# Two attention branches on one core: scaling phi(Q) on GpSimd in place of dividing numerators on VectorE

## The chip, the cores and the metric

The kernel runs on one core of a Trainium2 chip. The metric is the device time of one execution in microseconds (us). A core has five engines that each run their own stream of instructions in order: TensorE (PE, with the loading of weights as PEld), VectorE (DVE), ScalarE (ACT), GpSimd (POOL) and SyncE (SP), which here issues DMAs. They wait for each other through semaphores: `s_pe`, `s_dve`, `s_act` and `s_pool` count an engine's finished work, and `s_n5`, `s_n6`, `s_q0` and their like count landed DMAs.

## The reference, cut to what matters

Input x is 2048 x 512 with 32 heads of 16. Branch A is softmax attention. Branch B is linear attention with phi. A gate per token mixes them.

```python
g = sigmoid((x * gate_w).sum(-1, keepdims=True))
# A
scores = einsum("bhqd,bhkd->bhqk", q, k) * Dh ** -0.5
a = (softmax(scores) @ v) @ A_wo
# B: phi(t) = where(t > 0, t + 1, exp(t)) + 1e-6
kv = einsum("bhsd,bhse->bhde", phi(k), v)
z = einsum("bhsd->bhd", phi(k))
num = einsum("bhqd,bhde->bhqe", phi(q), kv)
den = einsum("bhqd,bhd->bhq", phi(q), z)[..., None] + 1e-6
b = (num / den) @ B_wo
return g * a + (1 - g) * b
```

## The kernel before, in words

**Branch A** is 32 rounds (a group of 8 heads, a quarter of 512 queries, and one of two halves of the heads) of 64 units each. A unit is the scores of 128 keys by 512 queries for one head. TensorE makes the scores in PSUM (`ps<-Qpad,KT`), and there are two ways on. ScalarE exponentiates two or three units with one instruction (`PT<-ps`, 128x1024 or 128x1536), and each result goes into one product with V (`ps<-PT,Vaug`). Or VectorE converts one unit to a 16-bit integer whose bits read as a rough power of two (`DP<-ps`, a "claimed" unit), and four such units are taken together to be shifted twice by a constant: this is GpSimd's 64-bit integer add (`DP<-DP`, INT64_ADD). A claimed unit thus gives three products with V (`ps<-DP,Vaug`), one from VectorE's write and two from GpSimd's. Products of a round add up in one PSUM bank, which VectorE evicts to `oraw`; small DMAs and a reciprocal normalise it.

**Branch B** fills gaps. `step_BK` makes phi(K) by blocks of 128 tokens, `step_Z` sums it, `step_M` and `step_KV` give the block-diagonal KV of each head, `step_gate` the gate. For each quarter of the queries (`qc`) `step_BQ` makes phi(Q) transposed, `step_den` the denominators with tokens on partitions, and `step_num` the numerators of 128 tokens, which VectorE divides while it evicts them (`OB<-ps,rdB`); a transposing DMA per 128 tokens turns the result (`obt`) for the output product. `step_out` and `step_pre` multiply both branches with the output weights into one bank, and VectorE scales by g.

**What sets the order.** The whole order is laid down when the kernel is built. A planner goes through ScalarE's groups one by one with estimated durations (`POOL_TT = 1.3`, `POOL_ADD = 1.09` and others) and puts other work on TensorE between two groups' scores; a table `ORDER` gives, for every 8 groups, the planner's options. Nothing is decided at run time: each engine runs its list, and a late result holds whoever stands in front of it and all that is queued behind.

**GpSimd's libraries.** The built order has, besides INT64_ADD, rows that read only `ISA`: each reloads the library from which GpSimd takes its operations. The build puts one ahead of an operation that is not in the library loaded last. Before the change there is one, ahead of the first INT64_ADD; the trace has it as two records named MODIFY_POOL_CONFIG.

Of the kernel before, what the change touches and what calls it, by code (L numbers as in the profile page):

```python
# [22 lines left out]
class K:  # L23
# [31 lines left out]
    "000000000000000000000000",  # L55
    "000000000000000000000000",
    "000000000000000000000000",
    "000000000000000000000000",
    "000000000000000000000000",
    "000000000001000000000000",  # L60
    "000000200201000000000000",
    "000000000000000000000000",
    "000000000000000000000000",
    "000000200000000000100000",
    "000000000000000000000002",
    "000000000000000000000000",
    "000000000000000000000000",
    "000000000000000000002001",
    "010000001000000000000000",
    "000000200000000000000000",  # L70
    "000000000000000000000000",
    "000000000000000000000000",
    "000000000000000000000000",
    "000001000200000000000000",
    "000001000200020000000000",
    "000000200000000000000000",
    "000000000001000000000000",
    "000000030000000000000000",
    "000000030001000000000000",
    "000000000002000000000000",  # L80
    "100000200002000000000000",
    "000000000000000000000000",
    "000100200000000000100000",
    "000100200100000001100000",
    "000000030000000000000000",
    "000020030002001000000000",
    "000020000000000000000000",
    "000020000100000000000000",
    "000000000000000000000000",
    "000010000000001000000003",  # L90
    "200010000000001000000003",
    "000000000000000000000000",
    "000000000000000000000000",
    "000000100000000000000000",
    "000002020000000000000000",
    "000000000000000010000000",
    "000000000000020000000000",
    "000020000000020000020000",
    "000000000000000000000000",
    "000000000001000001000000",  # L100
    "000000000000000000000002",
    "000000000000000000000000",
    "000000000000000000000000",
    "000000002000200001000000",
    "010000202000200011002000",
    "000000000000020000001000",
    "000000000100200000000000",
    "200020000000000000100000",
    "200020200000100000200000",
    "200020200100100000001000",  # L110
    "000000010100000000000000",
    "000000000000000000000000",
    "000000000000000010000010",
    "000000000002000010000010",
    "000000000000000000000000",
    "000000000000000000000000",
    "000000000000000010000000",
    "000000100000000000000000",
    "010000100000000000200000",
    "000000000000000000020010",  # L120
    "000000000110000000000000",
    "200000000100010000000000",
    "000000200000010000000000",
    "000000002000000000000000",
    "000000012000000000000000",
    "000000000000000000000001",
    "010001000000000000000000",
    "000000000000000100000000",
    "000000000100000000000000",
    "300000000200000000000000",  # L130
    "000000000000000000000000",
    "000020200000010000000000",
    "200020200000010000200000",
    "000000000002000000000000",
    "000000000001010000000000",
# [130 lines left out]
class _Res:  # L266

    __slots__ = ("name", "w", "r", "tw", "tr", "we", "pend", "pw")

    def __init__(self, name):  # L270
        self.name = name
        self.w = None
        self.r = {}
        self.tw = 0.0
        self.tr = 0.0
        self.we = None
        self.pend = 0
        self.pw = 0

# [58 lines left out]
def bass_gated_mix__mha_block__linear_attn_block__prompt_kernel(  # L338
# [33 lines left out]
    with ExitStack() as es:  # L372
# [66 lines left out]
        Zsel = SB([128, NCC, 8], BF16, "Zsel")  # L439

        phiK = SB([128, 2, 4, D], BF16, "phi")
        phiQT = phiK

        xnat = phiQT[:].rearrange("p a i n -> p (a i n)").rearrange("p (b c) -> p b c", b=NTB)
        rdB = SB([128, 2, 128], FP32, "rdB")

        OB = SB([128, 4, D], BF16, "OB")
        MT = OB
# [4 lines left out]

        def obt(tb):
            if tb < NTB // 2:
                return wB[:, :, D + 128 * tb:D + 128 * (tb + 1)]
            return OBT2[:, :, 128 * (tb - NTB // 2):128 * (tb + 1 - NTB // 2)]
# [6 lines left out]
        wide = OB[:].rearrange("p a n -> p (a n)").bitcast(FP32)[:, 0:512]  # L464
# [29 lines left out]
        semN = [SEM(f"s_n{k}") for k in range(5)]  # L494
        n_counts = [0] * 5
        semOB = [SEM(f"s_ob{b}") for b in range(NTB)]
# [9 lines left out]
        r_wA, r_warm, r_wB, r_woA, r_woB = R("wA"), R("warm"), R("wB"), R("woA"), R("woB")  # L506
# [8 lines left out]
        r_PT = [R(f"PT{i}") for i in range(NPT)]  # L515
        r_DP = [[R(f"DP{i}{k}") for k in range(NTRI)] for i in range(NB)]
# [15 lines left out]
        r_phiQT = r_phiK  # L532
        r_rdB = [R("rdB0"), R("rdB1")]
        r_OB = [R(f"OB{i}") for i in range(4)]
        r_OBT = [R(f"OBT{b}") for b in range(NTB)]
# [5 lines left out]
        r_wide = r_OB[0:2] + r_MT  # L541
# [49 lines left out]
        def blocker(it, reads, writes):  # L591
            for other in sorted((x for x in items if x.seq < it.seq), key=lambda x: x.seq):
                if any(conflicts(o, reads, writes) for o in other.ops):
                    return other
            return None
# [44 lines left out]
        def settle(reads, writes):  # L640

            while True:
# [212 lines left out]
        for t in range(1, NQC):  # L855
# [5 lines left out]
        op(PO, lambda: nc.gpsimd.memset(gw[:], 0.0), writes=[r_gw], dur=0.1)  # L861
        dma(gw[:, :, 0:1], gate_w.rearrange("(cc p o) -> p cc o", p=128, o=1), semG, writes=[r_gw], total_after=16, noncontig=True, E=SP,
            lands=8)
        xt_all = [r_xT[c][t] for c in range(NCC) for t in range(NQC)]
# [45 lines left out]
        op(PO, lambda: nc.gpsimd.memset(ones32[:, 0:1], 1.0), writes=[r_ones32], dur=0.1)  # L910
        op(PO, lambda: nc.gpsimd.memset(dev[:], OK_MID), writes=[r_dev], dur=0.2)
# [21 lines left out]
        def bank_ap(b):  # L933
            return ps[:, 512 * b:512 * (b + 1)]
# [154 lines left out]
        def row_to_columns(dst, sem, r_dst):  # L1089

            settle(r_wide, r_dst)
            st = est_start(SP, r_wide, r_dst)
            deps = _deps_for(r_wide, r_dst)
            for j in range(4):
                SP.add(lambda j=j: nc.sync.dma_start(dst(j), wide[32 * j:32 * j + 1, :]), deps, inc=False, dma_sem=sem, dma_val=64)
            SP.t = st + 0.59 * 4
            for res in r_wide:
                res.r[id(sem)] = _Raw(sem, 64)
                res.tr = max(res.tr, SP.t + 4.0)
            for res in r_dst:  # L1100
                res.w = _Raw(sem, 64)
                res.r = {}
                res.tw = SP.t + 4.0
                res.we = None

        def step_gate(**kw):
            rd = xt_all + [r_gw]

            def pieces(b):
                o = bank_ap(b)  # L1110
                fns = [[f_row(o, j, gw[:, cc, :], xT[:, cc, 512 * j:512 * (j + 1)], start=(cc == 0), stop=(cc == NCC - 1))
                        for j in range(4)] for cc in range(NCC)]
                return [(fns[k] + fns[k + 1], rd, 2 * MM512, 2 * MM512, "cols") for k in (0, 2)]

            def post(b):
                def moved():
                    row_to_columns(lambda j: eg[:, 4 * j:4 * j + 4], semRow[0], [r_eg])
# [1413 lines left out]
```

## Time and profile before

| what | value |
|---|---|
| median of 3 runs | 656.64 us (656.3 to 656.82) |
| span of the profiled execution | 655.0 us (the runs' median is 1.6 more) |
| ScalarE busy | 641.3 us, 98% |
| TensorE busy | 637.0 us, 97% |
| VectorE busy | 577.0 us, 88% |
| GpSimd busy | 366.6 us, 56% |
| INT64_ADD on GpSimd | 345, of 1.04 us |

In the profile's rows a group reads: line, engine, operation, out<-in, shapes, count, then busy time and the mean ns of one, then the idle time ahead of it and who ended it. A row of waits reads: who waited, for whom, us in total, times, longest. `POOLq` and `SPq` are the engines' instruction sequencers. TensorE's busy time counts overlapping ends of matmuls, so 97% is not the share of its peak. Line 826 is the helper that issues every matmul.

### The profile page before, as it was taken

The numbers are of one execution on the slowest core, as the hardware profiler recorded it, in microseconds if no ns is written. First come the engines' busy times: TensorE is split into PE (matmuls) and PEld (weight loads), VectorE is DVE, ScalarE is ACT, GpSimd is POOL, SyncE is SP. The second block draws the span as 40 slices with busy tenths as digits, with TensorE's granted clock in tenths as the row PEclk, the third lists the DMA queues.
The fourth block names the chain that finished last, engine by engine and source line by source line (L and its number), as shares of the span: only waits on it lengthen the run. The fifth ranks groups of instructions, "written<-read, shape, count | busy, mean of one in ns | idle before, by whom it ended". The sixth has DMA issues, their size and how long they took to land.

```text
span 655.0 us, 18894 instructions
## 1 busy us (share of the span) xinstructions
PE 637.0 (97%) x7881; PEld 188.3 (29%) x7881; DVE 577.0 (88%) x994; ACT 641.3 (98%) x702; POOL 366.6 (56%) x365
## 2 busy tenths in 40 slices
PE   8999999999999999999999999999999999999997
PEld 4322222332223233233222233232222222222223
DVE  6588999989888887999999999999989989879984
ACT  5999999999999999999999999999999999999995
POOL 6055566555565554544474656566767656646650
PEclk9999999999999999999999999999999999999999
DMA  9900101001022010101202002020101001010111
GB/s 212 272 6 8 29 3 32 6 11 28 3 56 46 15 23 3 35 11 28 41 11 45 16 15 39 17 53 11 27 11 27 19 23 39 18 43 19 43 26 38
DMA packets 45968, 22.97 MB, mean 35 GB/s; under 512 B 35128, under 2 KB 41720, under 8 KB 45880
## 3 DMA queue, kind: packets, MB, share of 16 engines
q1 hardware_dynamic: 43864, 20.14, 13.9%
q10 hardware_dynamic: 2016, 1.57, 0.9%
q8 instruction: 65, 1.06, 0.7%
q14 instruction: 23, 0.19, 0.1%
HBM read 8.00 MB, written 2.10 MB: 15 GB/s over the span
## 4 chain that ended last, share of the span: by engine, by line
ACT 81%; PE 18%; DVE 0%; issue 0%; POOL 0%; ACTq 0%; POOLq 0%
ACT PT L2239 79%; PE ps L826 17%; ACT epool L1136 2%; PE ps L833 0%; DVE DP L2341 0%; DVE Qpad L1035 0%; DVE KT L1007 0%; DVE DP L2346 0%; DVE flag L2351 0%; POOL warm L871 0%; POOL gw L861 0%; POOL dummy L843 0%; ACT eg L1121 0%; ACTq L2454 0%; POOLq L2516 0%
## 5 line engine op out<-in xcount | busy, mean ns | idle before, releaser
L2239 ACT ACTIVATE PT<-ps 128x1024 bf16<-128x1024 f32 (+1 forms) x662 | 632.1, 1211 | 1.2 <-PE ps L826 0.9
L1790 POOL INT64_ADD DP<-DP x345 | 355.3, 1040 | 267.3 <-DVE DP L1746 201.1
L1746 DVE TENSOR_SCALAR DP<-ps 128x512 int16<-128x512 f32 x694 | 451.6, 683 | 42.4 <-PE ps L826 37.1
L826 PE MATMUL ps<-Qpad,KT 32*128 32x512 bf16 x2048 | 261.6, 384 | 11.3 <-ACT PT L2239 5.4
L826 PE MATMUL ps<-DP,Vaug 128*32 128x512 f16 x2077 | 200.2, 384 | 0.0
L826 PE MATMUL ps<-PT,Vaug 128*32 128x512 bf16 x1344 | 156.9, 384 | 1.0 <-DVE oraw L1475 0.5
L826 PEld LDWEIGHTS ps<-Qpad,KT 32*128 32x128 bf16 x2048 | 66.4, 91 | 282.9 <-ACT PT L2239 258.5
L826 PEld LDWEIGHTS ps<-DP,Vaug 128*32 128x32 bf16 x2077 | 47.1, 95 | 61.7 <-issue 42.8
L826 PEld LDWEIGHTS ps<-PT,Vaug 128*32 128x32 bf16 x1344 | 36.6, 94 | 44.2 <-issue 36.1
L826 PE MATMUL ps<-xT,wA 128*32 128x512 bf16 x432 | 33.0, 384 | 0.0
L1136 ACT ACTIVATE epool<-ps 128x512 bf16<-128x512 f32 x32 | 26.2, 817 | 0.0
L1475 DVE COPY oraw<-ps 128x512 f32<-128x512 f32 x31 | 21.1, 680 | 1.0 <-PE ps L826 1.0
L826 PE MATMUL ps<-warm 128*32 128x512 bf16 (+1 forms) x113 | 20.4, 401 | 1.2 <-POOL warm L871 1.2
L826 PE MATMUL ps<-wB,xT 128*32 128x512 bf16 x256 | 19.7, 384 | 0.0
L826 PE MATMUL ps<-xT,wB 128*32 128x512 bf16 x256 | 19.1, 384 | 0.0
L826 PE MATMUL ps<-woA,OT 128*32 128x512 bf16 (+1 forms) x226 | 18.9, 384 | 0.0
L1141 DVE SCALAR_TENSOR_TENSOR phi<-ps,epool 128x512 bf16<-128x512 f32 x24 | 16.5, 686 | 0.5
L1139 DVE TENSOR_SCALAR epool<-epool 128x512 bf16<-128x512 bf16 x32 | 9.3, 292 | 6.7 <-ACT epool L1136 6.3
L1007 DVE CAST KT<-ps 128x512 bf16<-128x512 f32 (+1 forms) x16 | 10.7, 666 | 5.2 <-PE ps L826 5.2
L826 PE MATMUL ps<-wA,xT 128*128 128x128 bf16 x192 | 14.9, 220 | 0.0
L1062 DVE CAST Vaug<-ps 128x512 bf16<-128x512 f32 x16 | 10.9, 682 | 2.3 <-PE ps L826 2.3
L826 PEld LDWEIGHTS ps<-wA,xT 128*128 128x128 bf16 x192 | 10.8, 98 | 5.4 <-issue 4.5
(115 smaller groups left out, 224.0 us busy)
## 6 DMA issues: line engine op xcount, KB each, us to landing
rbc<-oraw SPq DMA_DIRECT2D x16, 256.0 KB
OT<-in_A_x_dram SPq DMA_DIRECT2D x4, 512.0 KB, 7.3
Qpad<-Qs SPq DMA_DIRECT2D x124, 16.0 KB, 1.8
oraw<-oraw SPq DMA_DIRECT2D x60, 32.0 KB, 1.9
wA<-in_A_wqkv_dram SPq DMA_DIRECT2D x1, 1536.0 KB, 7.9
wB<-in_B_wqkv_dram SPq DMA_DIRECT2D x1, 1536.0 KB, 8.9
out_dram<-outt SPq DMA_DIRECT2D x12, 128.0 KB, 1.7
phi<-in_A_x_dram ACTq DMA_DIRECT2D x3, 256.0 KB, 6.0
```

The source lines that it names most:

```text
L826: return lambda: nc.tensor.matmul(o, lhsT=l, rhs=r, start=start, stop=stop, skip_group_check=sg)
L1007: push(1, [(lambda: nc.vector.tensor_copy(KT[:, par, c0:c1], src), [r_bank[b]], [r_KT[par][t]], d_psum(n), None)])
L1062: ops = [(lambda: nc.vector.tensor_copy(v_group(NQC * par + v)[:, :, :, 0:16], src), [r_bank[b]], [r_V[par][v]], d_psum(512), lambda: v_do ...
L1136: op(AC, lambda: nc.scalar.activation(epool[:, s, :], bank_ap(b), ACT.Exp), reads=[r_bank[b]], writes=[r_e[s]], dur=0.6, issue=0.48)
L1139: (lambda: nc.vector.tensor_scalar(epool[:, s, :], epool[:, s, :], 1.0, 1e-6, op0=ALU.min, op1=ALU.add), [r_e[s]], [r_e[s]], 0.29, None),
L1141: (lambda: nc.vector.scalar_tensor_tensor(out=dst, in0=bank_ap(b), scalar=0.0, in1=epool[:, s, :], op0=ALU.max, op1=ALU.add), [r_bank[b], ...
L1475: push(0, [(lambda: nc.vector.tensor_copy(oraw[:, half, :], acc), [r_acc], [r_oraw[half]], d_psum(512), evicted)])
L1746: push((0 if in_group else 1) + K.PRIO_NEW, [(lambda: nc.vector.tensor_scalar(DP[:, i, 512 * k:512 * (k + 1)].bitcast(I16), bank_ap(b), FR ...
L1790: ops = (*ops[:4], None, POOL_ADD, lambda z=z, i2=i2, i=i, n=n: nc.gpsimd.int64_add(DP[:, i2, 0:n].bitcast(I64), DP[:, i, 0:n].bitcast(I64 ...
L2239: op(AC, lambda p0=p0, b0=b0, n=n: nc.scalar.activation(PT[:, 512 * p0:512 * p0 + n], ps[:, 512 * b0:512 * b0 + n], ACT.Exp, scale=LN2 / F ...
```

## The change

1. `step_num`, its 16 evictions and the 16 transposing DMAs are gone. In their place KV is formed transposed (`step_KV` swaps its operands) and multiplied into the output weight once (`step_W`, four products, written back over `woB`). The output product then takes phi(Q) itself, scaled.
2. `step_den` makes the denominators with heads on partitions (32 x 128, four column groups). VectorE adds the epsilon, inverts and multiplies by the gate's exponential into `rdc`. Four DMAs gather it into `rows_` (in `MT`'s space), four more spread each head's row over its 16 partitions (`rdb`, in phi(K)'s space, so rows of it read `phi<-MT`). GpSimd then multiplies phi(Q) by it in place: 4 instructions a quarter, 16 in all, of 128x512 bf16.
3. phi(Q) of the four quarters lies where K's and V's weights of branch B were (`wB`) and where phi(K)'s second half was (`OBT`), each in its own space.
4. The gate's exponential is one 128x512 instruction from PSUM in place of a 128x16 one, with the tokens laid out by another map (`gcol`).
5. `ORDER` is another table of the same size. The rest (`blocker`, `settle`, counting in thirds of a unit without fractions) is the planner's own bookkeeping.

```diff
 ORDER = [
-    "000000000000000000000000",
...
+    "010000030000100010000000",
...
-        Zsel = SB([128, NCC, 8], BF16, "Zsel")
+        Zsel = SB([128, NCC, 32], BF16, "Zsel")
...
+        def phiq(qc):
+            if qc < NQC // 2:
+                return wB[:, :, D + 512 * qc:D + 512 * (qc + 1)]
+            return OBT2[:, :, 512 * (qc - NQC // 2):512 * (qc + 1 - NQC // 2)]
...
-                    fns = [f_mm(o[:, 128 * i:128 * (i + 1)], MT[:, cc, 128 * i:128 * (i + 1)],
-                                wB[:, cc, 2 * D + 128 * i:2 * D + 128 * (i + 1)], start=(cc == 0), stop=(cc == NCC - 1))
+                    fns = [f_mm(o[:, 128 * i:128 * (i + 1)], wB[:, cc, 2 * D + 128 * i:2 * D + 128 * (i + 1)],
+                                MT[:, cc, 128 * i:128 * (i + 1)], start=(cc == 0), stop=(cc == NCC - 1))
...
+        def step_W(i, **kw):
+            rd = [r_KVbd, r_woB[i]]
+
+            def pieces(b):
+                return [(f_cols(bank_ap(b), KVbd[:, i, :], woB[:, i, :]), rd, MM512, MM512, "cols")]
+
+            def post(b):
+                push(1, [(lambda: nc.vector.tensor_copy(woB[:, i, :], bank_ap(b)), [r_bank[b]], [r_woB[i]], d_psum(512), None)])
+            return Step(pieces, post, reads=rd, **kw)
...
         def step_den(qc, **kw):
...
+                return [([f_mm(o[32 * m:32 * m + 32, 0:128], Zsel[:, i, :], phiq(qc)[:, i, 128 * m:128 * (m + 1)],
+                               start=(i == 0), stop=(i == NCC - 1), sg=True) for i in range(NCC) for m in range(4)],
+                         rd, 0.25, 0.1, "cols")]
...
+                def inverted():
+                    ndma(5, [(rows_[0:32, 128 * m:128 * (m + 1)], rdc[32 * m:32 * m + 32, :]) for m in range(4)], r_rdB[1:], r_wide)
+                    ndma(6, [(rdb[:, p, i, :], parts(rows_, 8 * i, [[1, 8]], [[0, 16], [1, 512]])) for i in range(NCC)],
+                         r_wide, r_rdb[p])
+                    for i in range(NCC):
+                        push(1, [(lambda i=i: nc.gpsimd.tensor_tensor(phiq(qc)[:, i, :], phiq(qc)[:, i, :], rdb[:, p, i, :], ALU.mult),
+                                  [r_rdb[p][i], r_PQ[qc][i]], [r_PQ[qc][i]], 0.0, None, POOL_TT)])
...
-        def step_num(tb, **kw):
...
-                    dma(obt(tb), OB[:, s, :], semOB[tb], reads=[r_OB[s]], writes=[r_OBT[tb]] + r_wBkv[tb:tb + 1] + (r_phi2 if tb == NTB // 2 else []),
-                        total_after=16, transpose=True, lands=4.0)
-                push(1, [(lambda: nc.vector.tensor_tensor(dst, src, rv, ALU.mult), [r_bank[b], r_rdB[p]],
-                          [r_OB[s]] + (r_MT if tb < 4 else []),
-                          d_psum(512), after)])
...
-        b_steps += [step_gate(), step_Z()] + [step_M(c) for c in range(NCC)] + [step_KV()] + first_q
+        b_steps += [step_Z()] + [step_M(c) for c in range(NCC)] + [step_KV(), step_gate()]
+        b_steps += [step_W(i) for i in range(NCC)]
```

On GpSimd, in the middle of the program, where before 345 sums stand in one row, the order is now this. `DP<-DP` are INT64_ADDs, TENSOR_TENSOR the multiplications by 1/den (of the first quarter in `wB`, later ones in `OBT`), a bare `ISA` a reload of the library.

```order
-L1790 ISA DP<-DP 128x1024 x345
```

```order
+L1794 ISA DP<-DP 128x1024 x216
+L1266 ISA
+L1266 TENSOR_TENSOR wB<-wB,phi 128x512 x4
+L1794 ISA
+L1794 ISA DP<-DP 128x1024 x15
+L1266 ISA
+L1266 TENSOR_TENSOR wB<-wB,phi 128x512 x4
+L1794 ISA
+L1794 ISA DP<-DP 128x1024 x10
+L1266 ISA
+L1266 TENSOR_TENSOR OBT<-OBT,phi 128x512 x4
```

A fourth place of the same form follows after 12 sums, and 93 sums stand behind it. Each four multiplications now have a reload ahead of them and another behind.

On TensorE, before, a numerator (`KVbd,phi`) stands between a score group and the products of that round:

```order
L826 MATMUL ps<-Qpad,KT 128x512 [waits s_dve,s_act,s_q2]
L826 MATMUL ps<-Qpad,KT 128x512 x2
L826 MATMUL ps<-KVbd,phi 128x128 [waits s_dve]
L826 MATMUL ps<-KVbd,phi 128x128 x3
L826 MATMUL ps<-DP,Vaug 32x512 [waits s_pool]
```

After, at the first of the four places, this is where TensorE takes the first sum that GpSimd makes behind the second reload. The row with `s_pool` waits for that sum and stands ahead of the next score group:

```order
L840 MATMUL ps<-xT,wB 32x512 x8
L840 MATMUL ps<-Qpad,KT 128x512 [waits s_dve,s_act]
L840 MATMUL ps<-Qpad,KT 128x512 x2
L840 MATMUL ps<-PT,Vaug 32x512 x9
L840 MATMUL ps<-DP,Vaug 32x512
L840 MATMUL ps<-PT,Vaug 32x512 x2
L840 MATMUL ps<-DP,Vaug 32x512 x4
L840 MATMUL ps<-Qpad,KT 128x512 [waits s_dve,s_act]
L840 MATMUL ps<-Qpad,KT 128x512 x2
L840 MATMUL ps<-DP,Vaug 32x512 [waits s_pool]
L840 MATMUL ps<-DP,Vaug 32x512 x4
```

The numerators are gone from between the scores; the products that wait for GpSimd stand as before, now with the multiplications and reloads queued ahead of some of the sums they wait for.

On SyncE's queue, before, at the first quarter's numerators:

```order
L733 DMA_TRANSPOSE wB<-OB 128x4x128 [waits s_dve] x3
L775 DMA Qpad<-Qs 16x512 [waits s_dve]
L775 DMA Qpad<-Qs 16x512 x7
L775 DMA rsum<-oraw 128x1x16 [waits s_dve]
L775 DMA oraw<-oraw 16x512 [waits s_n0]
```

After, at the first quarter's denominators:

```order
L789 DMA Qpad<-Qs 16x512 x7
L789 DMA rsum<-oraw 128x1x16 [waits s_dve]
L789 DMA MT<-rdB 32x128 [waits s_dve]
L789 DMA MT<-rdB 32x128 x3
L789 DMA phi<-MT 128x1x512 [waits s_n5]
L789 DMA phi<-MT 128x1x512 x3
L789 DMA rsum<-oraw 128x1x16 [waits s_dve]
```

The transposing DMAs are gone; eight plain DMAs a quarter have come, the second four behind a wait for the first four's landing.

On ScalarE the built order has 613 exponentials of 128x1024 and 42 of 128x1536, where before there are 630, 31 and one of 128x512.

More of the change, by code (lines that the diff above doesn't have):

```diff
@@ L136 @@
+    "000000000000200000000000",
 ]
@@ L640, in settle @@
         def settle(reads, writes):
-            while True:
+            while any(res.pend for res in writes) or any(res.pw for res in reads):
                 hit = None
```

341 lines of the change are left out of this document (162 added, 179 removed).

## The prediction

> **What bounds the kernel now.** I read the page first: engine shares, then the chain that ended last, then the groups.
>
> ```profile
> span 655.0 us, 18894 instructions
> PE 637.0 (97%) x7881; PEld 188.3 (29%) x7881; DVE 577.0 (88%) x994; ACT 641.3 (98%) x702; POOL 366.6 (56%) x365
> ...
> ACT 81%; PE 18%; DVE 0%; issue 0%; POOL 0%; ACTq 0%; POOLq 0%
> ...
> L2239 ACT ACTIVATE PT<-ps 128x1024 bf16<-128x1024 f32 (+1 forms) x662 | 632.1, 1211 | 1.2 <-PE ps L826 0.9
> L1790 POOL INT64_ADD DP<-DP x345 | 355.3, 1040 | 267.3 <-DVE DP L1746 201.1
> ```
>
> ScalarE's 662 exponentials fill the span and ScalarE waited 1.2 us for anything in front of them; the chain goes through it for 81%. So the time is a count of ScalarE instructions by their pitch, plus every moment in which TensorE has no scores ready for ScalarE. GpSimd and VectorE have room. The pitch comes from the chain in order of time (start us, us, what):
>
> ```profile
> 1.16 4.02 PE ps L826 x9
> ...
> 10.95 4.14 ACT PT L2239 x3
> ...
> 68.88 0.49 ACT epool L1136
> ...
> 401.36 106.77 ACT PT L2239 x116
> ```
>
> The stretch of 116 gives 106.77/116 = 0.92 us for a 128x1024 exponential (I call one a group), the first three give 4.14/3 = 1.38 for a 128x1536 one, and a 128x512 one takes 0.49. Next, who waited for whom, which shows how TensorE hangs on the others:
>
> ```profile
> PEld ps L826 <- ACT PT L2239: 258.8, 584, 1.1
> POOL DP L1790 <- DVE DP L1746: 201.1, 143, 17.5
> ...
> PEld ps L826 <- POOL DP L1790: 8.2, 33, 0.4
> ```
>
> TensorE waits for GpSimd's sums 33 times, never over 0.4 us, because its own lead over ScalarE is of that size: before almost every score group it waits for ScalarE to free a bank (584 waits, 0.44 us on average). A wait for GpSimd longer than that comes out on ScalarE.
>
> **The change, part by part.** *ScalarE.* The built order has 613 instead of 630 exponentials of 1024, 42 instead of 31 of 1536, none instead of one of 512; one 128x512 exponential for the gate replaces a tiny one. By the pitches above: -17 x 0.92 + 11 x 1.38 - 0.49 + 0.49 = -0.5 us. VectorE takes 696 instead of 694 units, so the time that it is spared goes nearly unused.
>
> *VectorE and TensorE.*
>
> ```profile
> L1267 DVE TENSOR_TENSOR OB<-ps,rdB 128x512 bf16<-128x512 f32 x16 | 10.9, 680 | 0.2 <-PE ps L826 0.2
> ...
> L1245 DVE TENSOR_TENSOR rdB<-rdB,gom 128x128 f32<-128x128 f32 x4 | 1.1, 279 | 0.0
> ```
>
> The 16 numerator evictions go (-10.9 us), four casts of KVW come (4 x 0.68 = 2.7). Numerators' and narrow denominators' matmuls go (16 x 4 and 4 x 16), four products with the output weight and four wide denominators come. All this lies beside ScalarE, which does not wait for VectorE: 0 in the sum, and no worse than 0 since it only shrinks.
>
> *SyncE.* Sixteen transposing DMAs at 1.26 us of queue go; per quarter 4 + 4 plain ones come, at 2.42 us for four:
>
> ```profile
> 348.05 1.26 SPq L733 DMA_TRANSPOSE wB<-OB  x1
> ...
> 350.01 2.42 SPq L775 DMA_DIRECT2D oraw<-oraw  x4
> ```
>
> ```profile
> oraw<-oraw SPq DMA_DIRECT2D x60, 32.0 KB, 1.9
> ```
>
> That is 20.2 against 8 x 2.42 = 19.4 us of queue. Behind the second four, which wait for the first four to land, stand the round's normalising DMAs; their result is wanted only by the output steps. Cost 0; if a Qpad load stood behind it, a wait of 1.9 us, the landing of such a small DMA, could show in each quarter: 8 us at most.
>
> *The end.* After the last exponential:
>
> ```profile
> 646.85 0.67 PE L826 MATMUL ps<-Vaug,PT 128*128 128x52 bf16 x20
> ...
> 647.36 0.56 PE L826 MATMUL ps<-Vaug,DP 128*128 128x52 bf16 x16
> ```
>
> 36 such matmuls stand there, 1.07 us; the new order leaves 12 to 36 for it. I take 12: -0.7 (at worst 0).
>
> *GpSimd.* Here is the price. The sixteen multiplications themselves: INT64_ADD reads 1024 words a partition in 1.04 us, and the multiplication reads 2 x 512 elements, so 1.04 each, four in a row 4.2 (bounds: VectorE's 0.68 for a two-operand product, and 2.08 if each operand costs a pass). But the built order has an operand-less instruction ahead of each four and another ahead of the sum behind them: eight switches of GpSimd's instruction library, where the kernel before has one. Its trace shows that one by records on GpSimd's sequencer:
>
> ```profile
> L1790 POOLq MODIFY_POOL_CONFIG  x2: 11/11/11, 15.5 to 15.6; - x2
> ...
> 32.27 0.68 DVE L1746 TENSOR_SCALAR DP<-ps 128x512 int16<-128x512 f32 x1
> ...
> 33.05 2.06 POOL L1790 INT64_ADD DP<-DP  x2 [17.54 <-DVE DP L1746]
> ```
>
> The record is 0.02 us, but the first sum starts only at 33.05, 0.10 us behind the VectorE write that it needs (32.27 + 0.68), which is the usual lag. So the load took anything from 0 to 17.5 us, out of sight. A library has to come from memory; the nearest rows are the program's plain loads from HBM, issue to landing. Of nine these are the shortest, the middle and the longest, and the smallest in size:
>
> ```profile
> PT<-in_A_x_dram ACTq DMA_DIRECT2D x1, 512.0 KB, 4.0
> ...
> woA<-in_A_wo_dram SPq DMA_DIRECT2D x1, 512.0 KB, 6.2
> ...
> wB<-in_B_wqkv_dram SPq DMA_DIRECT2D x1, 1536.0 KB, 8.9
> ...
> gw<-in_gate_w_dram SPq DMA_DIRECT2D x1, 1.0 KB, 7.5
> ```
>
> I take L = 6.2 us a switch, with 4.0 and 8.9 as its likely bounds. That 1 KB takes 7.5 and 512 KB 4.0 says that size does not decide.
>
> The Trainium skill, page "GPSIMD Engine Reference", section 2.1 "Instruction dispatch", says that the first call after a library load pays about 6 us (5.95 measured) with no instruction in the profile; no run shown here has that price. By it the sum below would be 703.
>
> What the switches push back: GpSimd runs in order, and so does TensorE, whose next product with a sum stands ahead of the next scores. At each of the four places I counted, in the built order, the groups from the one whose scores release the last sum ahead of the first switch to the one ahead of whose scores TensorE takes the first sum behind the second: 10, 12, 14 and 10. Two of these groups go for VectorE's write at the front and TensorE's products and scores at the back (a trace sample of the front: VectorE's write of 0.69 us and then the sums at once):
>
> ```profile
> 339.52 1.91 DVE L1746 TENSOR_SCALAR DP<-ps 128x512 int16<-128x512 f32 x3
> ...
> 341.53 2.06 POOL L1790 INT64_ADD DP<-DP  x2 [0.38 <-DVE DP L1746]
> ```
>
> So GpSimd has 8, 10, 12 and 8 groups: 7.4, 9.2, 11.0 and 7.4 us. It has to do 1, 2, 2 and 1 sums, a switch, four multiplications, a switch and one more sum: 2 x 6.2 + 4.2 + 1.04 x (2, 3, 3, 2) = 18.7, 19.7, 19.7, 18.7. ScalarE stands for the difference: 11.3 + 10.5 + 8.7 + 11.3 = 41.8 us. Nothing gives it back, as ScalarE has no idle time to catch up from. The denominators' DMAs are no further wait: VectorE's result for them stands 11 to 16 groups ahead of that last sum, at least 10 us, and two lots of four take 2 x (2.42 + 1.9) = 8.6 us to issue and land.
>
> *TensorE's rate after each stand.* At the program's start the first nine 128x512 matmuls took 4.02 us, 0.45 each, and the next sixteen of 128 columns 1.75; near the end four of 512 took 1.02, 0.26 each:
>
> ```profile
> 4.97 1.75 PE L833 MATMUL ps<-identb,PT 128*128 128x128 bf16 x16
> ...
> 641.73 1.02 PE L826 MATMUL ps<-woB,OBT 128*128 128x512 bf16 x4
> ```
>
> TensorE thus starts at half rate for 4.0 to 5.6 us. If a stand of 10 us puts it back there, its work per group, 98 of 100 us in this stretch, no longer fits in 0.92 us:
>
> ```profile
> 380.00:480.00 100.00, 98.05 (x1175) 28.50 (x1167) 96.57 (x165) 100.00 (x112) 63.75 (x62) 1.00 0.14 26
> ```
>
> (the columns are span, PE, PEld, DVE, ACT and POOL busy, then granted clock and DMA). Half of 4.0 us lost is 2.0 a place, 8.0 in all; bounds 0 (the work counts filler matmuls) and 2.8 a place.
>
> The Trainium skill, "TensorE: Matmul & The Clock Gate", Part 1, "What's actually happening", has the clock halved after an idle window of about 3.4 us and restored after as long a busy one; that would be 1.7 a place and the total 704. The trace before has no such stand to agree or differ.
>
> **The sum.** -0.5 - 0.7 + 41.8 + 8.0 = +48.6 on a span of 655.0: 703.6. The runs' median is 656.64, 1.6 above the span for what lies around it: **705 us**.
>
> **Rivals.** *The switch is nearly free*, as its 0.02 us records say: the tails alone remain, 656.6 - 1.2 = 655.4, just faster. Against it: a record on the sequencer says nothing of what the cores behind it do. It decides below L = (7.4 - 2.1 - 4.2)/2 = 0.6 us a switch at the first and last place, 1.0 and 1.8 at the others; above 0.6 each 0.1 costs some 0.4 us at first, 0.8 in the end.
> *Only one switch of each pair loads* (say the multiplication is resident and its switch empties nothing): 12.5 us of work instead of 18.7 at the first place; stands of 5.1, 4.3, 2.5 and 5.1 = 17.0, and with half-rate starts 656.6 - 1.2 + 17.0 + 8.0 = 680. For it: ahead of its one load, at 15.5 us, GpSimd ran even a cast without any:
>
> ```profile
> 7.68 0.29 POOL L903 CAST blockmask<-maskK 128x128 bf16<-128x128 f32 x1
> ```
>
> Against it: the built order has both switches in the same form.
> *The load is as long as its cover*, 17.5 us: 8 x 11.3 more, 795. Only that upper bound speaks for it.
>
> **Chances.** Main case 0.77, one load of each pair 0.11, free switch 0.08, long load 0.04. The main case's range: L of 4.0 without half rate, 705 - 17.6 - 8.0 = 679; L of 8.9 with 2.8 a place, 705 + 21.6 + 3.2 = 730. I widen it by two microseconds at the bottom for the single load: 678 to 730, which leaves out the free switch, the long load and a little of the main case. This kernel's measurement can tell about 0.2% (1.3 us) from no change. Only the free switch is not clearly slower; it divides into faster 0.03, same 0.03 and slower 0.02: so 0.03, 0.03, 0.94.
>
> **What will show it.** Right: pairs of MODIFY_POOL_CONFIG ahead of the multiplications' line and behind it; GpSimd empty for about 6 us behind each pair; four waits of TensorE for GpSimd of 8 to 12 us, one a place, between 385 and 500 us of the span (shifted by the earlier ones); ScalarE idle some 42 us more, in four gaps; a granted clock under 1.00 only there. The pitch of the exponentials outside the gaps stays 0.92 us, and the stretch before 380 us and the one behind the last place run as before. Wrong: no gap behind the records; or gaps that end at the DMAs' landing rather than at GpSimd; or TensorE waiting for GpSimd in places far from the multiplications, which would make the one-operand price wrong; or waits of SyncE's queue reaching the Qpad loads.

## The result and the profile after

The changed kernel takes 706.05 us (705.06 to 707.94) against 656.73 us (656.3 to 656.91) for the kernel before on the same chip: a ratio of 1.0757, 95% interval 1.0742 to 1.0773. The forecast was 705.0, range 678 to 730, with 0.94 for slower.

From the page of the changed kernel: span, busy shares, the slices of ScalarE and of TensorE's clock, the chain, and three groups.

```profile
span 704.2 us, 18879 instructions
...
PE 642.6 (91%) x7878; PEld 185.6 (26%) x7878; DVE 572.6 (81%) x983; ACT 642.3 (91%) x695; POOL 385.3 (55%) x383
...
ACT  6999999999999999999999984949392999999996
...
PEclk9999999999999999999999996978795999999999
...
ACT 53%; PE 31%; issue 7%; POOL 4%; DVE 4%; DMA 1%; SPq 1%; POOLq 0%; ACTq 0%
...
L2239 ACT ACTIVATE PT<-ps 128x1024 bf16<-128x1024 f32 (+1 forms) x655 | 631.0, 1200 | 50.4 <-PE ps L840 50.1
...
L1266 POOL TENSOR_TENSOR OBT<-OBT,phi 128x512 bf16<-128x512 bf16 x8 | 9.4, 1197 | 13.8 <-DVE DP L1750 7.0
L1266 POOL TENSOR_TENSOR wB<-wB,phi 128x512 bf16<-128x512 bf16 x8 | 9.0, 1146 | 13.9 <-issue 13.9
```

ScalarE's exponentials do as much as before (631.0 us against 632.1), but ScalarE now waits 50.4 us ahead of them, against 1.2. The 49 us are these waits. They lie in four holes between 410 and 545 us, and TensorE's clock falls below full speed in the same slices.

The waits (who, for whom, us in total, times, longest) show the next link:

```profile
DVE DP L1750 <- PE ps L840: 93.5, 146, 11.9
PEld ps L840 <- POOL DP L1794: 55.8, 50, 11.9
ACT PT L2239 <- PE ps L840: 50.1, 17, 11.7
PE ps L840 <- POOL DP L1794: 43.5, 4, 11.6
POOL DP L1794 <- issue: 23.8, 4, 6.1
```

ScalarE waits for TensorE, and TensorE for GpSimd's sums, four times by 11 us. Ahead of these sums GpSimd itself waits for nothing that the profile shows ("issue"), up to 6.1 us at a time. Its timeline (start us, us, what, idle before) at the first and the third place:

```profile
410.62 1.04 POOL L1794 INT64_ADD DP<-DP  x1 [1.29 <-DVE DP L1750]
418.63 4.46 POOL L1266 TENSOR_TENSOR wB<-wB,phi 128x512 bf16<-128x512 bf16 x4 [6.98 <-issue]
429.19 6.11 POOL L1794 INT64_ADD DP<-DP  x6 [6.09 <-issue]
...
495.72 4.93 POOL L1266 TENSOR_TENSOR OBT<-OBT,phi 128x512 bf16<-128x512 bf16 x4 [7.02 <-DVE DP L1750]
506.47 3.06 POOL L1794 INT64_ADD DP<-DP  x3 [5.82 <-issue]
```

Each switch of the library has two records of only 1 to 13 ns, as the instructions by line show (shortest/median/longest in ns; the second row includes the two of the program's first load):

```profile
L1266 POOLq MODIFY_POOL_CONFIG  x8: 11/12/13, 411.6 to 523.0; - x8
L1794 POOLq MODIFY_POOL_CONFIG  x10: 1/4/11, 19.6 to 534.4; - x10
```

Behind the records GpSimd stands empty: 6.98, 6.95, 7.02 and 6.79 us ahead of the multiplications, 6.09, 5.79, 5.82 and 6.06 us ahead of the sums behind them. At the third place the profile names a VectorE write as what ended the 7.02 us; the wait is as long as at the other three places, so it is read here as the switch too. A multiplication takes 1.14 us (the median), four 4.46 to 4.93.

What TensorE and ScalarE did at the first place:

```profile
418.31 0.39 PE L840 MATMUL ps<-Qpad,KT 32*128 32x512 bf16 x3
430.27 1.03 PE L840 MATMUL ps<-DP,Vaug 128*32 128x512 f16 x5 [11.57 <-POOL DP L1794]
...
431.25 0.61 PE L840 MATMUL ps<-Qpad,KT 32*128 32x512 bf16 x3
...
435.51 0.39 PE L840 MATMUL ps<-Qpad,KT 32*128 32x512 bf16 x3
```

```profile
418.04 2.12 ACT L2239 ACTIVATE PT<-ps 128x1024 bf16<-128x1024 f32 x2
431.91 1.02 ACT L2239 ACTIVATE PT<-ps 128x1024 bf16<-128x1024 f32 x1 [11.74 <-PE ps L840]
433.42 1.02 ACT L2239 ACTIVATE PT<-ps 128x1024 bf16<-128x1024 f32 x1 [0.49 <-PE ps L840]
434.93 5.71 ACT L2239 ACTIVATE PT<-ps 128x1024 bf16<-128x1024 f32 x6 [0.49 <-PE ps L840]
```

TensorE stands 11.57 us for the first sum behind the switch. Then its score matmuls run at 0.61 us for three, instead of 0.39, until 434.8 us, and ScalarE's groups follow at 1.51 us (431.91, 433.42, 434.93) instead of 0.9. From the starts of ScalarE's instructions, each less the 0.904 us of an undisturbed group, the four stands are 12.1, 10.6, 10.7 and 11.7, together 45.0 us, and the slow groups behind them (2, 3, 3 and 3, by some 0.6) 6.6 us. That is 51.6 us; the rest of the change must then have gained some 2 us.

### The profile page after: what moved, and what is told of

It reads as the page before. It is cut to its first block, busy times and chain, and to the rows that moved or that the text cites. A ratio compares the mean times of both kernels' runs of the same rounds, so it can differ in the third digit from the quotient of the medians.

```text
span 704.2 us, 18879 instructions
## 1 busy us (share of the span) xinstructions
PE 642.6 (91%) x7878; PEld 185.6 (26%) x7878; DVE 572.6 (81%) x983; ACT 642.3 (91%) x695; POOL 385.3 (55%) x383
## 4 chain that ended last, share of the span: by engine, by line
ACT 53%; PE 31%; issue 7%; POOL 4%; DVE 4%; DMA 1%; SPq 1%; POOLq 0%; ACTq 0%
ACT PT L2239 51%; PE ps L840 31%; DVE DP L1750 2%; POOL OBT L1266 1%; ACT epool L1149 1%; POOL wB L1266 1%; POOL DP L1794 1%; DMA phi<-MT 1%; SPq L789 1%; DMA MT<-rdB 0%; DVE oraw L1479 0%; ACT MT L1134 0%; DVE rdB L1271 0%; DVE Qpad L915 0%; DVE epool L1152 0%
## 5 line engine op out<-in xcount | busy, mean ns | idle before, releaser
L2239 ACT ACTIVATE PT<-ps 128x1024 bf16<-128x1024 f32 (+1 forms) x655 | 631.0, 1200 | 50.4 <-PE ps L840 50.1
L840 PE MATMUL ps<-Qpad,KT 32*128 32x512 bf16 x2048 | 264.4, 389 | 11.5 <-ACT PT L2239 7.0
L840 PE MATMUL ps<-DP,Vaug 128*32 128x512 f16 x2085 | 207.5, 390 | 44.1 <-POOL DP L1794 43.5
L840 PE MATMUL ps<-PT,Vaug 128*32 128x512 bf16 x1333 | 165.2, 388 | 0.0
L1149 ACT ACTIVATE epool<-ps 128x512 bf16<-128x512 f32 x32 | 24.5, 765 | 0.0
L840 PE MATMUL ps<-warm 128*32 128x512 bf16 (+1 forms) x133 | 22.8, 435 | 1.0 <-POOL warm L885 1.0
L1266 POOL TENSOR_TENSOR OBT<-OBT,phi 128x512 bf16<-128x512 bf16 x8 | 9.4, 1197 | 13.8 <-DVE DP L1750 7.0
L1266 POOL TENSOR_TENSOR wB<-wB,phi 128x512 bf16<-128x512 bf16 x8 | 9.0, 1146 | 13.9 <-issue 13.9
L1022 DVE CAST KT<-ps 128x512 bf16<-128x512 f32 (+1 forms) x16 | 10.6, 664 | 5.2 <-PE ps L840 5.2
L840 PEld LDWEIGHTS ps<-wA,xT 128*128 128x128 bf16 x192 | 11.3, 100 | 5.8 <-issue 4.5
```

The costliest lines, as they stand in the source:

```text
L840: return lambda: nc.tensor.matmul(o, lhsT=l, rhs=r, start=start, stop=stop, skip_group_check=sg)
L1022: push(1, [(lambda: nc.vector.tensor_copy(KT[:, par, c0:c1], src), [r_bank[b]], [r_KT[par][t]], d_psum(n), None)])
L1149: op(AC, lambda: nc.scalar.activation(epool[:, s, :], bank_ap(b), ACT.Exp), reads=[r_bank[b]], writes=[r_e[s]], dur=0.6, issue=0.48)
L1266: push(1, [(lambda i=i: nc.gpsimd.tensor_tensor(phiq(qc)[:, i, :], phiq(qc)[:, i, :], rdb[:, p, i, :], ALU.mult), [r_rdb[p][i], r_PQ[qc][i ...
L2239: op(AC, lambda p0=p0, b0=b0, n=n: nc.scalar.activation(PT[:, 512 * p0:512 * p0 + n], ps[:, 512 * b0:512 * b0 + n], ACT.Exp, scale=LN2 / F ...
```

## The experiments

The theory to be tested: each of eight switches empties GpSimd for 6 to 7 us, TensorE stands for the sum behind, ScalarE for TensorE, and TensorE starts again at half rate. Rivals: the newly laid order or the denominators' DMAs hold TensorE up whatever GpSimd does; the multiplications, not the switches, are the cost; the slow groups have another cause than the stands.

**No switch: copies in place of multiplications.**

```diff
-nc.gpsimd.tensor_tensor(phiq(qc)[:, i, :], phiq(qc)[:, i, :], rdb[:, p, i, :], ALU.mult)
+nc.gpsimd.tensor_copy(phiq(qc)[:, i, :], rdb[:, p, i, :])
```

> The changed kernel with each of GpSimd's sixteen multiplications replaced by a copy of 1/den into the same block of phi(Q); the scaling is left out. Order of all engines, DMAs and waits are those of the changed kernel; a copy needs no switch of the library, so the seven switches behind the first sums' own are gone too. The theory (eight switches of 6 to 7 us and four multiplications of 4.5 us a place): the stands go, and with the 1.2 us of smaller terms it comes to 655 to 657 us. Rival 1 (the newly laid order or the denominators' DMAs make TensorE wait, whatever GpSimd does there): over 690. Rival 2 (GpSimd's 512-column work itself is too long at these places, a copy of about 1 us being as bad as a multiplication): 670 to 690.

Measured: 658.36 us (657.2 to 659.97), ratio 1.0023 (1.0013 to 1.0034). With the same order and the same DMAs, but without the eight switches (the expectation's seven is a miscount), 47.7 of the 49.3 us are gone. The first rival falls, and the second as far as copies of 0.62 us can tell. But it is 1.4 us above the upper end of what was expected, and a little slower than the kernel before: there is one gap of its own, which the last experiments below take up.

**Switches without the multiplications' length: 8 columns instead of 512.**

```diff
-nc.gpsimd.tensor_tensor(phiq(qc)[:, i, :], phiq(qc)[:, i, :], rdb[:, p, i, :], ALU.mult)
+nc.gpsimd.tensor_tensor(phiq(qc)[:, i, 0:8], phiq(qc)[:, i, 0:8], rdb[:, p, i, 0:8], ALU.mult)
```

> The changed kernel with multiplications of 8 columns instead of 512 (the scaling of the other 504 is left out), all eight switches kept, the order the same. The theory says that the multiplications' own time is 4.5 of the 23 us that GpSimd needs at a place: four times some 4 us less, 688 to 692 us. The rival that the multiplications are the main cost and the switches a minor one: under 670. The rival that only the switches count and the rest was hidden: 704 to 707.

Measured: 689.86 us (689.36 to 690.36), as the theory has it. GpSimd's timeline of this kernel at the first place:

```profile
418.94 0.68 POOL L1266 TENSOR_TENSOR wB<-wB,phi 128x8 bf16<-128x8 bf16 x4 [6.94 <-issue]
425.49 6.11 POOL L1794 INT64_ADD DP<-DP  x6 [5.88 <-issue]
```

The idle times of 6.94 and 5.88 us stay when the work between them is 0.68 instead of 4.46 us. The time falls by 16.2 us, 4.05 a place. So the switches cost the same whatever is done between them, and the multiplications' own time is on the path too, since nothing else fills the room.

**One place alone.**

```diff
-push(1, [(lambda i=i: nc.gpsimd.tensor_tensor(phiq(qc)[:, i, :], phiq(qc)[:, i, :], rdb[:, p, i, :], ALU.mult),
+push(1, [(lambda i=i: nc.gpsimd.tensor_tensor(phiq(qc)[:, i, :], phiq(qc)[:, i, :], rdb[:, p, i, :], ALU.mult) if qc == 3
+          else nc.gpsimd.tensor_copy(phiq(qc)[:, i, :], rdb[:, p, i, :]),
```

> The changed kernel with multiplications in the last quarter alone; the other three quarters copy 1/den instead (their scaling is left out) and so need no switch. Two switches are left of eight. If the places are independent and nothing is given back later, a quarter of the loss is left and 0 or a little from the smaller terms: 655.5 + 11.7 + 1.9 = 669 us. If the loss is not made place by place (a later place pays for an earlier one's lateness, or the first switch is the dear one): under 662 or over 680.

Measured: 671.03 us (670.65 to 671.42), 12.7 us above the copies alone and 2 us above the expected 669. Four such places are 50.7, against 47.7 that the four together cost over the copies; the last place is one of the two longer ones. So the loss is made place by place: the one switch pair costs about its quarter, and nothing of it is given back in the 150 us behind it.

**The clock: TensorE kept at work through the stands.**

```diff
+# ahead of the first product that waits for a sum behind a place
+for k in range(46):
+    PE.add(f_mm(acc_of(acc_bank[0]), warm[:], warm4, start=False, stop=False, sg=True), ...)
```

> The changed kernel with 46 filler matmuls of 512 columns on TensorE (9.9 us at full rate), which need nothing from GpSimd, ahead of the first product that waits for a sum behind each of the four places, so that TensorE works through the stand. If the two or three groups at 1.5 instead of 0.92 us behind each stand come from TensorE running at half rate after idling, they go back to 0.92 and the time falls by 4 to 6.6 us, to 699.5 to 702, with the granted clock near 1.00. If those groups are late for another reason (sums that follow the switch one by one), no change: 705 to 707. If the fillers end behind the sum, it is slower by what they run over.

Measured: 698.28 us (697.0 to 699.5), 7.8 us less, with a granted clock of 0.999 instead of 0.959. TensorE, then ScalarE, at the first place:

```profile
418.75 10.10 PE L847 MATMUL ps<-warm 128*128 128x512 bf16 x46
430.05 0.60 PE L847 MATMUL ps<-DP,Vaug 128*32 128x512 f16 x5 [1.19 <-POOL DP L1801]
...
430.60 0.39 PE L847 MATMUL ps<-Qpad,KT 32*128 32x512 bf16 x3
```

```profile
418.16 2.12 ACT L2246 ACTIVATE PT<-ps 128x1024 bf16<-128x1024 f32 x2
431.03 8.36 ACT L2246 ACTIVATE PT<-ps 128x1024 bf16<-128x1024 f32 x9 [10.75 <-PE ps L847]
```

The scores take 0.39 at once, nine groups follow without a wait, and ScalarE's stand is 10.75 instead of 11.74 us: the first group behind the stand had paid for the half rate as well. The four stands sum to 42.4 us here instead of 45.0. So of the 51.6 us, 42.4 are the stands for GpSimd at full rate and 7.8 TensorE's rate; 1.4 lie between the two ways of counting. It was outside the expected 699.5 to 702 because the expectation counted the slow groups alone.

**A switch with cover.** The kernel before with one small product on GpSimd ahead of its first sum, where it stood 17.5 us idle:

```diff
+op(PO, lambda: nc.gpsimd.tensor_tensor(O_sb[:, 0, 0:8], O_sb[:, 0, 0:8], O_sb[:, 0, 8:16], ALU.add), reads=[r_O], writes=[r_O], dur=0.1)
```

> The kernel before the change with one further product of two tensors of 8 columns on GpSimd, on zeroed memory, ahead of its first sum: one more pair of switches, at the program's start, where GpSimd sat idle for 17.5 us. The theory, by which a switch costs what GpSimd needs to load a library and holds up nothing else: some 13 us fit into the 17.5, the first sum still starts near 33 us, and the time is that of the kernel before, within 0.2%. If a load holds up DMAs or other engines, or takes longer at the start, where the input loads run: slower by 1 us or more.

Measured: 656.37 against 656.39 us, ratio 0.9998 (0.9989 to 1.0008): no difference. GpSimd's timeline:

```profile
25.63 0.19 POOL L913 TENSOR_TENSOR Osb<-Osb 128x8 bf16<-128x8 bf16 x1 [10.10 <-issue]
33.24 2.06 POOL L1791 INT64_ADD DP<-DP  x2 [7.42 <-DVE DP L1747]
```

Two loads fit into the old gap, and the first sum is 0.2 us later than before (33.05). Here the switches cost nothing: nothing behind them on GpSimd came late, and no other engine was held up.

**Room made for the switches.** The planner told 7.0 us more for the first multiplication of a quarter and 6.0 more for the last:

```diff
-                                  [r_rdb[p][i], r_PQ[qc][i]], [r_PQ[qc][i]], 0.0, None, POOL_TT)])
+                                  [r_rdb[p][i], r_PQ[qc][i]], [r_PQ[qc][i]], 0.0, None, POOL_TT + (7.0 if i == 0 else 6.0 if i == NCC - 1 else 0.0))])
```

> The changed kernel, its multiplications on GpSimd, with the planner told what was measured: 7.0 us more for the first multiplication of four and 6.0 us more for the last. It lays the order anew: 69 exponentials of 1536 and 590 of 1024 instead of 42 and 613, that is 27 x 1.331 - 23 x 0.904 = 15 us more work on ScalarE, and the third and fourth quarter's multiplications stand together, so that three pairs of switches are left. If the stands were only there because the order left GpSimd 8 to 12 groups for some 23 us, the long waits of TensorE for GpSimd go and ScalarE's count is what is left: 668 to 676 us. If switches cost something that room cannot hide (another engine held up while a library loads): over 685.

Measured: 683.2 us (682.68 to 683.73), above what was expected. In this order branch B's output is not the reference's, and why is not known, so the run serves for its waits alone. The long waits for GpSimd are gone, as the first of these rows shows:

```profile
PEld ps L840 <- POOL DP L1794: 8.3, 36, 0.4
...
PEld ps L840 <- DVE DP L1791: 8.1, 17, 0.6
```

So with room the switches no longer hold TensorE up. But the room is made at other engines' cost: ScalarE's larger count (some 15 us), and about 12 us of gaps in the same stretch, the longest of 3.76 us. For these the trace has a likely source. This order takes 42 sums off GpSimd (304 instead of 346) and has VectorE do the shifts itself (`DP<-DP`, line 1791: 26 instructions, 2 in the changed kernel). TensorE waits for them one by one (the second row), also just ahead of the ends of the two longest gaps, 3.58 and 3.76 us. How much of the 12 us is theirs was not measured.

**The multiplications on VectorE.** Four kernels: at GpSimd's old places; the same with the third quarter's broadcasts issued behind the round's first normalising DMA (`rsum<-oraw`); and the multiplications 12 VectorE items later, with that edit and without it.

```diff
-nc.gpsimd.tensor_tensor(phiq(qc)[:, i, :], phiq(qc)[:, i, :], rdb[:, p, i, :], ALU.mult)
+nc.vector.tensor_tensor(phiq(qc)[:, i, :], phiq(qc)[:, i, :], rdb[:, p, i, :], ALU.mult)
...
+HELDM.append((fn, reads, writes))        # the later ones: put off by 12 VectorE items
```

> The changed kernel with the sixteen multiplications on VectorE, at the places in the order at which GpSimd had them; TensorE's and ScalarE's orders and the DMAs are those of the changed kernel, and GpSimd is left with its sums and one library. The theory: no stand of 12 us; the run with copies came to 658.4 us, with one gap of about 4.5 us near 465 us, behind a reciprocal that waited for a DMA standing behind the four broadcasts of 1/den on SyncE's queue. If that gap comes from SyncE's queue it is here too, and the time is 657 to 660 us. If VectorE has no room for sixteen more products (it was busy 87% of the span), ScalarE waits for it in other places: 662 us or more.

> As the kernel before it in this list, with one further edit: in the third quarter alone the four DMAs that broadcast 1/den are issued behind the round's first normalising DMA instead of ahead of it; no other engine's order moves. If the gap near 465 us is the wait of VectorE's reciprocal for that DMA behind 5.8 us of broadcasts, it goes, and the time is 3 to 4.5 us below that kernel, 653 to 656 us, at or below the kernel before the change. If the gap is only the late end of something else (VectorE's own backlog), the two are the same.

> The multiplications on VectorE, with the edit on SyncE, and each multiplication 12 VectorE items later in its order, so that it finds 1/den landed; no other engine's order moves. The two runs with the multiplications on VectorE lost 9 us against the run with copies; the trace shows them waiting on VectorE for the broadcasts' DMAs, with TensorE's conversions queued behind. If that wait, and the half-rate groups behind it, is the whole of that loss: 653 to 657 us, at or below the kernel before. If VectorE has no room for sixteen products of 0.41 us: 660 us or more.

> The multiplications on VectorE, 12 VectorE items later, SyncE's order that of the changed kernel. Against the run before it in this list this tells the price of the third quarter's broadcasts on SyncE's queue alone: 4 to 5 us more than that run, 657 to 661 us. If the reciprocal's wait is not the cause, the two are the same.

Measured, in this order: 666.89 (ratio 1.0162, 1.0148 to 1.0177), 667.24 (1.016, 1.0147 to 1.0174), 664.98 (1.0139, 1.0124 to 1.0155) and 662.6 us (1.0099, 1.0084 to 1.0115). All beat the changed kernel, none the kernel before. None came out where its theory had it, and the edit on SyncE's queue gained nothing where 3 to 5 us were expected (with later multiplications it cost 2.4): in the second run VectorE stands 3.7 us at one multiplication for the broadcasts, which now land later. Against the copies the first lost 8.5 us. Later multiplications gained half of that, 4.3 us (666.89 to 662.6). In the first run's trace VectorE waits for the broadcasts 1.7 us in all, and TensorE falls to half rate twice; how the 4.3 us divide between these was not measured. The other 4.2 us go with VectorE's want of room. The run with copies and no third broadcast (below) has these busy times in the first place's stretch (PE, PEld, DVE, ACT, POOL, clock, DMA share):

```profile
410.00:430.00 20.00, 19.43 (x258) 6.00 (x255) 19.44 (x36) 20.00 (x24) 11.52 (x14) 1.00 0.17 35
```

VectorE is busy 19.44 of 20 us there, though 88% over the span. The last of the four runs has this in the same stretch:

```profile
410.00:430.00 20.00, 17.45 (x229) 5.43 (x222) 19.68 (x36) 18.55 (x21) 8.64 (x8) 1.00 0.18 36
```

ScalarE falls from 20.00 to 18.55 us. Over the four places (410 to 430, 440 to 460, 470 to 490 and 495 to 510 us) it is busy 4.1 us less than in the run with copies, about the 4.2 us that are left. There a multiplication can cost more than one instruction's time:

```profile
418.92 0.42 DVE L1302 TENSOR_TENSOR wB<-wB,phi 128x512 bf16<-128x512 bf16 x1
...
420.45 1.07 DVE L1302 TENSOR_TENSOR wB<-wB,phi 128x512 bf16<-128x512 bf16 x1
...
422.65 1.07 DVE L1302 TENSOR_TENSOR wB<-wB,phi 128x512 bf16<-128x512 bf16 x1
...
424.84 0.41 DVE L1302 TENSOR_TENSOR wB<-wB,phi 128x512 bf16<-128x512 bf16 x1
```

```profile
419.10 5.52 POOL L1830 INT64_ADD DP<-DP  x5 [0.78 <-DVE epool L1188]
```

The two that start while GpSimd's five sums run (419.10 to 424.62) take 1.07 us, the two outside 0.41 to 0.42. Of the sixteen, seven took 0.86 to 1.07, and each of them started while a sum ran; the other nine, at 0.41 to 0.42, did not.

**The gap in the run with copies.** Its SyncE queue, VectorE and ScalarE near 465 us:

```profile
454.06 5.80 SPq L789 DMA_DIRECT2D phi<-MT  x4
459.90 0.72 SPq L789 DMA_DIRECT2D rsum<-oraw  x1
```

```profile
463.87 0.35 DVE L1452 RECIPROCAL rraw<-rsum 128x32 f32<-128x32 f32 x1 [2.64 <-DMA rsum<-oraw]
```

```profile
465.57 1.02 ACT L2239 ACTIVATE PT<-ps 128x1024 bf16<-128x1024 f32 x1 [1.83 <-PE ps L840]
467.94 1.02 ACT L2239 ACTIVATE PT<-ps 128x1024 bf16<-128x1024 f32 x1 [1.34 <-PE ps L840]
469.88 1.02 ACT L2239 ACTIVATE PT<-ps 128x1024 bf16<-128x1024 f32 x1 [0.92 <-PE ps L840]
```

Four broadcasts of 1/den take 5.80 us of SyncE's queue. The DMA behind them is late, VectorE's reciprocal stands 2.64 us for it with TensorE's conversions queued behind, and ScalarE shows three gaps. First the broadcasts were issued behind that DMA:

```diff
+held.append(put) if hold else put()      # hold: the third quarter's four broadcasts
+while held and not hold:                 # the next batch of DMAs goes first
+    held.pop(0)()
```

> The run with copies in place of the multiplications (the scaling is left out, so no switch but the first), and the one edit on SyncE: in the third quarter the four DMAs that broadcast 1/den are issued behind the round's first normalising DMA instead of ahead of it; all other engines' orders are those of the run with copies. There GpSimd, not VectorE, waits for the broadcasts, so the later landing should hold up nobody. If SyncE's 5.8 us of broadcasts made the one gap of some 4.5 us near 465 us, it goes: 653.5 to 655.5 us, the 1.2 us or more below the kernel before that the exponentials and the end were to give. If that gap has another cause: 658 us as before.

Measured: 659.57 us (659.35 to 661.11), no gain; the expectation was wrong. The gap at 465 us is gone, but another DMA is late in its place. VectorE:

```profile
476.15 0.69 DVE L1472 TENSOR_TENSOR OT<-oraw,rbc 128x512 bf16<-128x512 f32 x1 [3.25 <-DMA rbc<-oraw]
```

Here the queue's time was not saved by another order; it was paid by what then stood behind. Then the four broadcasts were left out:

```diff
+if not skip:                             # skip: the third quarter's four broadcasts
     SP.add(lambda o=o, i=i: nc.sync.dma_start(o, i), deps, inc=False, dma_sem=sem, dma_val=total_after)
```

> The run with copies in place of the multiplications, with the four broadcasts of 1/den of the third quarter left out altogether (its copies take the first quarter's 1/den; no scaling anywhere, as before); every other instruction and its place is that of the run with copies. Issuing these broadcasts later only moved the gap from 465 us to 480 us, where VectorE then waited 3.3 us for the next round's DMA behind them. If the gap is the 5.8 us that they take of SyncE's queue, it now goes without a successor: 4 to 5 us less than the run with copies, 653 to 655 us, 2 to 3 us below the kernel before. If the new order of the third quarter is late by itself: 657 us or more.

Measured: 654.54 us (654.42 to 655.11), ratio 0.9971 (0.996 to 0.9982), clock 1.000. ScalarE through the place:

```profile
462.69 18.14 ACT L2247 ACTIVATE PT<-ps 128x1024 bf16<-128x1024 f32 x19
```

Nineteen exponentials without a gap that the profile shows. So the broadcasts of one quarter cost 3.8 us there, and the rest of the change (without switches, multiplications and this wait) gains 2.1 us. From 654.54, the changed kernel's 706.05 is 51.5 us more, which the four places' 51.6 account for. No version tried does the whole computation in less time than the kernel before.

## Why the prediction was right, step by step

*GpSimd, the main term.* Right. L was taken as 6.2 us a switch and is 6.9 us into the multiplication's library and 5.9 back, 6.4 on average. A multiplication was taken as 1.04 us and is 1.14. The stands were predicted as 11.3, 10.5, 8.7 and 11.3, 41.8 together, and are 42.4 at full rate, 45.0 with the first slow group in them. The third was the worst: 8.7 against 10.7. That L came from an HBM load's duration was luck in the choice of row; the bounds of 4.0 and 8.9 held it. That 41.8 and 42.4 lie so close is partly luck too, as two errors nearly cancel: in the run with fillers GpSimd's work at the four places takes 79.9 us instead of the predicted 76.8, and so the order left it some 37.5 us of room instead of 35.0. The Trainium skill's page "GPSIMD Engine Reference", section 2.1 "Instruction dispatch", has about 6 us (5.95) for the first call behind a load: the measured 5.9 us ahead of the sums agree, the 6.9 ahead of the multiplications are a microsecond longer.

*Half rate.* Right: 8.0 predicted, 7.8 taken away by the fillers. At the first place the slow matmuls last from 430.27 to 434.8 us, 4.5 us. The Trainium skill's page "TensorE: Matmul & The Clock Gate", Part 1, "What's actually happening", has the clock restored after at least one busy window of about 3.4 us. The 4.5 us measured here agree with "at least"; the prediction's 1.7 a place, an estimate from one such window, was too low, and 2.0 from the program's start the better price.

*ScalarE and the end.* The sum of -1.2 us was of the right sign and too small; the run without switches and without the third broadcasts gained 2.1. The pitch of 1.38 us for an exponential of 1536 is the whole extent of three in a row, 4.14 us, divided by three, which counts the end of the last one in full; undisturbed ones start 1.331 us apart, and those of 1024 0.904, by which the count alone gives -17 x 0.904 + 11 x 1.331 - 0.48 + 0.48 = -0.7. Behind the last exponential the changed kernel needs 7.7 us against 8.2, half a microsecond less. The other 0.9 were not traced.

*SyncE's queue.* This step failed, without showing in the total. Eight DMAs of 0.6 us were assumed (2.42 for four); the four that gather take about that, but the four broadcasts take 5.8 us. The wait was sought at the Qpad loads, as the normalising DMAs' result was held to be wanted only by the output steps. But VectorE runs its list in order and stands at the reciprocal for a normalising DMA behind the broadcasts, with TensorE's conversions queued behind; that costs 3.8 us at one place in the run with copies. In the changed kernel the stands cover it: no wait of VectorE for such a DMA is left there. The bound of 8 us had room for it. For the same reason the denominators' DMAs were closer to a wait than the prediction had it: at the first place the two lots take 10.4 us to issue alone (398.63 to 408.99), where 8.6 us to issue and land were reckoned. In the changed kernel the load ahead of the multiplications covers that; with copies GpSimd waits for them, 1.6 us the longest.

*VectorE has room.* Right for what the change left there, wrong as a general statement: by the 88% of the span it has, by the 19.44 of 20 us at the first place it has not. The prediction's own row for 380 to 480 us showed it, with VectorE busy 96.57 of 100 us. The multiplications moved there cost 4.2 us over the copies at best.

*The rivals.* The free switch falls by the idle times behind records of 12 ns; the single load of each pair by idle times on both sides; the long load by 7.0 us as the longest of the eight. The signs named for the main case appeared, the four waits of TensorE (11.9 us the longest) and the clock below 1.00 only there among them; ScalarE's idle time grew by 49 us and not by 42, as the waits ahead of the slow groups count in it.

## What to carry to other kernels

An operation that GpSimd takes from another library cost two loads wherever it stood between operations of the first, some 13 us here, however short it was; look for the records of the switch in the built order, not for their length in the trace, and ask whether the engines behind GpSimd have that much lead. On an in-order queue, changing who stands first moved the wait here and did not save it; leaving transfers out did. And whether an engine has room is read from the stretch in which the work is to stand, not from its share of the span.

## What the runs showed of the hardware beyond this

- Behind a switch of GpSimd's library in mid-program the engine stood empty 6.8 to 7.0 us towards the multiplications in the changed kernel (6.7 to 7.6 over the other runs with switches) and 5.8 to 6.1 towards INT64_ADD where nothing else held the sums. At the program's start, beside the input loads, it was 10.10 us.
- A copy on GpSimd needed no switch between INT64_ADDs and took 0.62 us for 128x512 where the multiplication takes 1.14.
- A 128x512 bf16 product of two SBUF operands on VectorE takes 0.41 us alone and up to 1.07 when it starts beside a sum of GpSimd.
- A DMA that spreads rows over 128 partitions held SyncE's queue 1.4 us (5.6 to 5.8 for four), one that gathers 32 rows 0.62 where nothing delayed it.
